# Value product of twelve chunks in four 64x64 tiles, with part sums in two PSUM banks

## The chip, the cores and the metric

The kernel runs on one core of a Trainium2 chip. The metric is the device time of one execution in microseconds (us). Before the change the median of three runs is 507.99 us (507.67 to 508.84).

## What is computed

An attention with a decaying state (RWKV), followed by a feed-forward layer with a gated activation. Cut to what matters:

```python
# r, k, v, w: (4, 8, 768, 48); u: (8, 48)
for t in range(768):
    cur = einsum('bhd,bhe->bhde', u * k[t], v[t])
    y[t] = einsum('bhd,bhde->bhe', r[t], state + cur)
    state = w[t][..., None] * state + einsum('bhd,bhe->bhde', k[t], v[t])
x = y as (3072 tokens, 384)
h = x @ w_in                      # 384 x 2048
out = (h / (1 + exp(-1.702 * h))) @ w_out   # 2048 x 384
```

## The kernel before

**Attention in chunks.** The 3072 tokens are cut into 24 chunks of 128 tokens (six chunks a batch entry). Inside a chunk the recurrence is turned into matrices. For each of the 8 heads there is a 128x128 matrix of scores, from a scaled k and a scaled r (`kf`, `qf`, products on rows of one head each, L359). A tile `am` holds for each head a diagonal matrix (L321, ScalarE) over which VectorE lays the scores where the key's token lies before the query's (`copy_predicated` with the mask `after`, L362). So `am` is triangular: keys on partitions, queries on columns, and of the four 64x64 quarters of each head's matrix the one with late keys and early queries is zero. The output of a chunk is `v` times `am`, plus the state of the chunks before times `qf`. It lies with a head's 48 features on partitions and tokens on columns.

**The crossed chunks.** From chunk 12 on (`CROSS`), heads come in pairs p = 0 to 3, and in the pairs 2 and 3 the two heads change places, so that products with the state (L371) run as four tiles of 64 rows by 64 columns of the PE array at once. Their eight products write two PSUM tiles `ps_c`, one for each half of the rows (`r_`), two pairs in each. The value products (L377) take all 128 rows (the keys) and half of the columns, two tiles at once, and add to the same banks. ScalarE then casts each `ps_c` tile to fp32r (`hi`, L222) and VectorE subtracts to get the rest (`lo`, L223), both into `x`. The output of the crossed pairs lies crossed in `x`. GpSimd's queue moves rows inside `x` by DMA (`fill_x`), and the feed-forward products of the lower half of the rows read `x` in another order (`first_rows`).

**The feed-forward in tasks.** Tokens come in six groups of four chunks (512 tokens), and each group has 16 tasks, one for each 128 of the 2048 hidden features: 96 tasks. A task's first product is 9 matmuls of 512 columns into a PSUM tile `ph`; ScalarE makes the gelu twice (`gh`, `gf`, L471), VectorE the difference `gl` (L472); two tasks later the second product adds 9 matmuls to the three output banks `po0` to `po2`. From task 32 on each matmul is cut into two halves of 64 rows that run side by side (`on_rows`, L512). At the end of a group ScalarE copies the three banks out (`ob`, L587, in the order bank 1, 0, 2), and only then can the next group's second product start in them; its first one starts in bank 1.

**What sets the order.** The order is written out by hand: a list of tokens up to task 32 (`RAMP`), and after that `rest()`, which places the steps of each chunk (`PARTS`) against the tasks, the same for every chunk: a new chunk every four tasks. Every engine then works in that order. A chunk's value products, its split and, for the chunk after it, the state update and the diagonals (`am`) fall in one place (step 8.5 of the one, 4.5 of the other). The chunks 16 and 20 have this place in the second task of a new group, and so just ahead of the copies `ob` of the group before.

Of the kernel before, what the change touches and what calls it, by code (L numbers as in the profile page):

```python
# [21 lines left out]
P = 128  # L22
# [4 lines left out]
C = P  # L27
# [57 lines left out]
def rwkv_ffn_kernel(ctx: ExitStack, tc, wkr, vp, vrk, ub, w_in, w_out, masks, vt, uc, out):  # L85
# [26 lines left out]
    after = cp.tile([P, C], F32, name="after")  # L112
# [5 lines left out]
    after_b = after.bitcast(I32).unsqueeze(1).broadcast_to([P, NP, C])  # L118
    u_heads = hm[:, 2:].rearrange("r (p h) -> r p h", h=2)
# [24 lines left out]

    def load(t):

        assert t < 2 or loaded.get(t - 2, [None])[0] is None
        a, v = lands[t % 2], values[t % 3]
        loaded[t] = [a[0:R2], v]
        first, last = (TOP if t == 0 else 0), (R2 if t % (NT - 1) == 0 else P)  # L150
        rows = wkr.rearrange("t r w -> (t r) w")[t * R + first - TOP : t * R + last - TOP]
        n = NP * CW + 1
        if t < CROSS:
            for c0, c1 in ((0, n), (n, a.shape[1])) if t < 2 else ((0, a.shape[1]),):
                if c0:
                    yield
                behind_moves(queue[0].dma_start(a[first:last, c0:c1], rows[:, c0:c1]))
        else:
            for c0, w in ((1, CW), (n, C), (n + NP * C, C)):
                for odd in range(2):  # L160
                    cols = slice(c0 + odd * 2 * w, c0 + (odd + 1) * 2 * w)
                    for half in range(2):
                        dst, src = TOP + half * D, (half ^ odd) * D
                        queue[0].dma_start(a[dst : dst + D, cols], wkr[t, src : src + D, cols])  # L164
        yield
        assert t < 3 or t - 3 in weighed
        queue[0].dma_start(v[:, TOP:], vrk[t, :, 0:DM])
        if t >= WHOLE:
            rk = pools["late"].tile([P, 2 * DM], F32, tag="rk", name="rk_t")
            queue[0].dma_start(rk, vrk[t, :, DM:])  # L170
            loaded[t].append(rk)
        yield
# [66 lines left out]
    def chunk(t):  # L239
# [7 lines left out]
        first, final = t % CB == 0, (t + 1) % CB == 0  # L247

# [24 lines left out]
        V.tensor_tensor(kf, k, li[:, :, 1:CW], op=ALU.mult)  # L273
# [37 lines left out]
        cross = t >= CROSS  # L311
# [49 lines left out]
        for h in range(2):  # L361
            V.copy_predicated(am[h], after_b, ps[h])  # L362
        yield
        cs = slice(col * C, (col + 1) * C)
        if cross:
            ps = [ps_a.tile([R2, 2, C], F32, tag="psa", name=f"ps_c{r_}") for r_ in range(2)]
            each = [(p, r_, r_ ^ p // 2) for p in (0, 2, 1, 3) for r_ in range(2)]
            if sf is not None:
                for p, r_, o in each:
                    c = p * D  # L370
                    T.matmul(  # L371
                        ps[r_][head(o), p % 2], sf[head(r_), c + o * TOP : c + HB], qf[head(r_), p],
                        start=p in (0, 2), stop=False, skip_group_check=True,
                    )
            for p, r_, o in each:
                c = (2 * p + o) * D
                T.matmul(  # L377
                    ps[r_][head(o), p % 2], v[:, c + o * TOP : c + HB], am[r_][:, p],
                    start=sf is None and p in (0, 2), stop=p in (1, 3), skip_group_check=True,
                )  # L380
# [39 lines left out]
    def fill_x(x, c0, c1, cross=False):  # L420

        for m in range(NM):
            for i, dst in enumerate((R2, 0)):
                j = TOP * (2 * m + i + 1)
                move = G.dma_start(  # L425
                    x[dst : dst + TOP, :, m ^ 2 * (cross and i == 0), c0:c1].bitcast(F32),
                    x[j : j + TOP, :, NM ^ 2 * (cross and j >= HB), c0:c1].bitcast(F32),
# [17 lines left out]
    def first_product(j, task):  # L445
# [5 lines left out]
        x = xs.get((i, 0), xs[i])  # L451
# [69 lines left out]
    def first_rows(j, half):  # L521
# [5 lines left out]
        for n in range(3 * NM):  # L527
# [5 lines left out]
                half, ("h", j), parts[j], w, xs[i][:, x, c ^ 2 * (half and starts[i] >= CROSS), cs],  # L533
# [47 lines left out]
    def store(i, start, N, order=range(NM)):  # L581
# [12 lines left out]
        xs.pop((i, 0), None)  # L594
# [5 lines left out]
    with tc.manual_schedule():  # L600
# [17 lines left out]
        def do(token):  # L618
# [7 lines left out]
            elif kind == "x":  # L626
                group, col = where[i]
                if col == CHUNKS[group] - 1:
                    fill_x(xs[group], 0, (col + 1) * C, i >= CROSS)
            elif kind == "c":  # L630
                x = xs[i, 0] = new_x(i)
                for c in range(NM):
                    for rows, src in ((slice(0, HB), c), (slice(HB, P), c ^ 2)):
                        G.dma_start(x[rows, :, c].bitcast(F32), xs[i][rows, :, src].bitcast(F32))
            elif kind == "u":
                nc.sync.dma_start(u_sb, ub)
                for x in crossed:
                    G.memset(x, 0.0)
            elif kind == "M":
# [19 lines left out]
        def rest():  # L659
# [18 lines left out]
            for j in range(FIRST, len(TASKS) + LAG):  # L678
                for post in range(2):
                    if post and j == len(TASKS) - WHOLE:  # L680
                        yield f"c{len(CHUNKS) - 1}"
# [140 lines left out]
```

## Time and profile before

| | before |
|---|---|
| median of three runs | 507.99 us |
| the profiled execution, its own time | 508.05 us |
| span of the profiled execution | 506.10 us |
| TensorE matmul busy (PE) | 494.2 us, 98% |
| VectorE (DVE) | 290.6 us, 57% |
| ScalarE (ACT) | 283.9 us, 56% |
| GpSimd (POOL) | 95.5 us, 19% |
| mean granted clock of TensorE | 0.997 of full speed |

The span is the stretch from the first to the last instruction; the execution's own time is 1.95 us longer. PE is TensorE's matmuls, PEld its loads of weights, which run beside the matmuls. An fp32 matmul shows as two rows in the trace (it runs in two passes), an fp32r matmul as one. Matmuls in different tiles of the array overlap, and a row's duration has the way through the array in it, so that the spacing of the starts and not the duration is the cost. Idle time counts where it lies on the engine that sets the end.

### The profile page before, as it was taken

How to read it: one execution, taken by the hardware profiler on the slowest of the kernel's cores; microseconds unless marked ns; L12 is line 12 of the kernel's file. 1: busy time of each engine (PE TensorE's matmuls, PEld its weight loads, DVE VectorE, ACT ScalarE, POOL GpSimd, SP SyncE). 2: the span in 40 equal slices, each digit the busy share in tenths (PEclk: the TensorE clock that was granted, in tenths of full speed). 3: DMA queues.
4: the chain of work that ended last, by engine and by line, in shares of the span. 5: the costliest groups of instructions: out<-in, count | busy, mean ns of one | idle time of the engine just before them, and what ended most of it. 6: DMA issues, size and time to landing. Idle time of an engine off the chain costs nothing.

```text
span 506.1 us, 11444 instructions
## 1 busy us (share of the span) xinstructions
PE 494.2 (98%) x4535; PEld 416.5 (82%) x4535; DVE 290.6 (57%) x451; ACT 283.9 (56%) x618; POOL 95.5 (19%) x200
## 2 busy tenths in 40 slices
PE   7999999999999999999999999999999999999994
PEld 3766777888888888888888888888888888888873
DVE  7899999999987213656456555555555322111210
ACT  4987889978865533465455465554564533323222
POOL 2002000000100200076304376303460002210000
PEclk9999999999999999999999999999999999999998
DMA  8996960125465300045112245111350001140001
GB/s 269 308 378 188 332 218 7 58 93 189 127 181 126 84 1 1 0 132 138 32 49 48 79 115 153 42 40 33 96 156 2 1 1 33 69 121 1 1 1 69
DMA packets 19471, 50.30 MB, mean 99 GB/s; under 512 B 4545, under 2 KB 8321, under 8 KB 19409
## 3 DMA queue, kind: packets, MB, share of 16 engines
q1 hardware_dynamic: 11664, 31.24, 19.3%
q0 software_dynamic: 7344, 17.72, 13.7%
q8 instruction: 38, 0.62, 0.5%
q10 hardware_dynamic: 400, 0.53, 0.3%
q14 instruction: 25, 0.20, 0.1%
HBM read 40.82 MB, written 4.72 MB: 90 GB/s over the span
## 4 chain that ended last, share of the span: by engine, by line
PE 82%; DVE 5%; ACT 4%; DMA 2%; issue 1%; POOL 1%; SPq 0%; ACTq 0%; DVEq 0%
PE po L512 26%; PE ph L512 24%; PE ps_s L359 3%; PE po L486 3%; PE ph L454 3%; PE po L487 3%; PE po L488 3%; PE ph L455 3%; PE ph L456 3%; PE ps_c L377 2%; DMA raw<-in_w_in 2%; PE ps_y L399 1%; PE ps_u L332 1%; PE ps_c L371 1%; PE ps_y L407 1%
## 5 line engine op out<-in xcount | busy, mean ns | idle before, releaser
L512 PE MATMUL ph<-x,pair 64*128 64x512 f32 x1134 | 185.5, 376 | 0.0
L472 DVE TENSOR_TENSOR gl<-gf,gh 128x512 fp32r<-128x512 f32 x96 | 66.3, 690 | 183.5 <-ACT gf L471 182.7
L512 PE MATMUL po<-gh,pair 64*128 64x512 f32 x768 | 157.6, 384 | 0.2 <-SPq L517 0.2
L512 PEld LDWEIGHTS ph<-x,pair 64*128 64x128 f32 x1134 | 143.5, 186 | 14.1
L471 ACT ACTIVATE gh<-ph 128x512 fp32r<-128x512 f32 x84 | 50.1, 597 | 157.7 <-PE ph L512 137.0
L512 PEld LDWEIGHTS po<-gh,pair 64*128 64x128 f32 x768 | 95.7, 186 | 10.4 <-issue 1.1
L512 PE MATMUL po<-gl,pair 64*128 64x512 f32 x384 | 99.2, 376 | 0.0
L425 POOL DMA_DIRECT2D x<-x x36 | 18.2, 512 | 248.5 <-DVE x L223 207.4
L321 ACT ACTIVATE am<-ident,s 128x128 f32<-128x128 f32 x192 | 58.8, 396 | 2.5 <-issue 1.5
L164 POOL DMA_DIRECT2D wkr_t<-in_wkr x108 | 53.8, 505 | 10.9 <-DVE kq L273 6.2
L512 PEld LDWEIGHTS po<-gl,pair 64*128 64x128 f32 x384 | 50.0, 186 | 4.8
L471 ACT ACTIVATE gf<-ph 128x512 f32<-128x512 f32 x84 | 49.8, 593 | 0.0
L454 PE MATMUL ph<-x,pair 128*128 128x512 f32 x99 | 39.0, 394 | 0.4 <-ACT gf L467 0.4
L456 PE MATMUL ph<-x,pair 128*128 128x512 f32 x99 | 38.0, 384 | 0.2 <-DVE pair L213 0.2
L455 PE MATMUL ph<-x,pair 128*128 128x512 f32 x99 | 37.9, 383 | 0.0
L486 PE MATMUL po<-gh,pair 128*128 128x512 f32 x96 | 37.8, 394 | 0.0
L488 PE MATMUL po<-gl,pair 128*128 128x512 f32 x96 | 36.9, 385 | 0.0
L487 PE MATMUL po<-gh,pair 128*128 128x512 f32 x96 | 36.8, 383 | 0.0
L228 ACT ACTIVATE junk<-lp 112x1032 bf16<-112x1032 f32 x24 | 25.6, 1068 | 12.3 <-DVE lp L258 12.2
L252 DVE TENSOR_TENSOR_SCAN lp<-wkr_t,d1r 112x516 f32<-112x516 f32 x24 | 29.4, 1225 | 1.3 <-DMA wkr_t<-in_wkr 1.0
L258 DVE TENSOR_TENSOR_SCAN lp<-wkr_t,d1f 112x516 f32<-112x516 f32 x24 | 29.4, 1225 | 0.1
L362 DVE COPY_PREDICATED am<-after,ps_s 128x512 f32<-128x512 int32 x40 | 26.9, 727 | 1.4 <-PE ps_s L359 1.2
(92 smaller groups left out, 645.0 us busy)
## 6 DMA issues: line engine op xcount, KB each, us to landing
wkr_t<-in_wkr SPq DMA_DIRECT2D x10, 770.5 KB, 5.3
raw<-in_w_out SPq DMA_DIRECT2D x6, 1024.0 KB, 11.4
raw<-in_w_in SPq DMA_DIRECT2D x5, 1024.0 KB, 10.9
wkr_t<-in_wkr POOLq DMA_DIRECT2D x72, 48.0 KB, 2.1
rk_t<-in_vrk POOLq DMA_DIRECT2D x9, 384.0 KB, 3.5
out_t<-ob POOLq DMA_DIRECT2D x12, 256.0 KB, 2.7
v_t<-in_vrk SPq DMA_DIRECT2D x15, 192.0 KB, 4.6
rk_t<-in_vrk SPq DMA_DIRECT2D x7, 384.0 KB, 3.4
```

The lines of the kernel that those rows point to most:

```text
L164: queue[0].dma_start(a[dst : dst + D, cols], wkr[t, src : src + D, cols])
L252: V.tensor_tensor_scan(li.rearrange("r p c -> r (p c)")[:, ::-1], w1[:, ::-1], d1r.rearrange("r p c -> r (p c)")[:, ::-1], 0.0, op0=ALU.mu ...
L321: A.activation(x_[:, p], ident, AF.Copy, scale=s[:, j : j + 1])
L454: T.matmul(o, h_, halves(x[:, 0, c, cs], plain), start=c == 0, stop=False)
L455: T.matmul(o, h_, halves(x[:, 1, c, cs], plain), start=False, stop=False)
L456: T.matmul(o, l_, halves(x[:, 0, c, cs], plain), start=False, stop=c == NM - 1)
L471: A.activation(g, ph, AF.Gelu_apprx_sigmoid, scale=1.0 / W_SCALE)
L472: V.tensor_tensor(gl, gf, gh.bitcast(F32), op=ALU.subtract)
L486: T.matmul(o, h_, halves(gh, plain), start=first, stop=False, skip_group_check=True)
L487: T.matmul(o, l_, halves(gh, plain), start=False, stop=False, skip_group_check=True)
L488: T.matmul(o, h_, halves(gl, plain), start=False, stop=f == NF - 1, skip_group_check=True)
L512: mm = T.matmul(by_twos(out), w[rows], halves(x[rows]), start=start, stop=stop, skip_group_check=True)
```

## The change

From chunk 12 on the value products are cut into tiles of 64 keys by one head's columns, four tiles at once, and the quarter that is zero is left out: for each pair and head one product of 128 columns and one of 64 instead of one of 128 columns over all keys. All products with the keys in one half of the rows write one bank, so `ps_c` is now a full bank for each half of the rows, and an output is the sum of two banks. So that both halves have the same work, the pairs 2 and 3 have their keys turned: the upper 64 tokens on the lower partitions. For this `kf` is written with its halves swapped, `am` starts from a turned diagonal (`turned`) and a mask of two halves (`after_x`), and `v`, `r` and `k` by tokens are loaded with their halves swapped for these pairs (`bring`, three DMAs for one). The heads' rows are loaded with six DMAs for twelve. The sum is made in `yt`: ScalarE copies half of the pairs from each bank, VectorE adds the parts of the other bank (four adds), and `split` works on the sum. `x` then has all heads in their places, so the crossed reads and the copy of the last group's `x` (token `c`, six DMAs) fall away. At token `u`, in the ramp, the new masks are made once.

```diff
@@ chunk(t), t >= CROSS
-        V.tensor_tensor(kf, k, li[:, :, 1:CW], op=ALU.mult)
+        if cross:
+            pairs_ = slice(0, NP // 2)
+            V.tensor_tensor(kf[:, pairs_], k[:, pairs_], li[:, pairs_, 1:CW], op=ALU.mult)
+            out_, *ins_ = (
+                y[:, NP // 2 :].rearrange("r p (b c) -> r p b c", b=2) for y in (kf, k, li[:, :, 1:CW])
+            )
+            V.tensor_tensor(out_[:, :, ::-1], *ins_, op=ALU.mult)
...
-                    A.activation(x_[:, p], ident, AF.Copy, scale=s[:, j : j + 1])
+                    A.activation(x_[:, p], turned if cross and p // 2 else ident, AF.Copy, scale=s[:, j : j + 1])
...
-            ps = [ps_a.tile([R2, 2, C], F32, tag="psa", name=f"ps_c{r_}") for r_ in range(2)]
+            ps = [ps_a.tile([R2, NP, C], F32, tag="psa", name=f"ps_c{r_}") for r_ in range(2)]
...
-            for p, r_, o in each:
-                c = (2 * p + o) * D
-                T.matmul(
-                    ps[r_][head(o), p % 2], v[:, c + o * TOP : c + HB], am[r_][:, p],
-                    start=sf is None and p in (0, 2), stop=p in (1, 3), skip_group_check=True,
-                )
+            for p, halves_ in ((0, (0, 1)), (2, (1, 0)), (1, (0, 1)), (3, (1, 0))):
+                for i_ in halves_:
+                    for r_ in range(2):
+                        o = r_ ^ p // 2
+                        c, rows, c0 = (2 * p + o) * D, slice(i_ * HB, (i_ + 1) * HB), HB * (i_ ^ p // 2)
+                        T.matmul(
+                            ps[i_][head(o), p, c0:], v[rows, c + o * TOP : c + HB], am[r_][rows, p, c0:],
+                            start=sf is None and p == 0, stop=p == 3, skip_group_check=True,
+                        )
...
+            yt = at.tile([R2, NP, C], F32, tag="rku", name="yt")
             for b, y in enumerate(ps):
-                split(*(xs[i][0:R2, n_, 2 * b : 2 * b + 2, cs] for n_ in range(2)), y)
+                two = slice(2 * b, 2 * b + 2)
+                A.copy(yt[:, two], y[:, two])
+            for b, y in enumerate(ps):
+                two = slice(2 - 2 * b, 4 - 2 * b)
+                for rows, cols in ((slice(0, HB), slice(HB, C)), (slice(HB, R2), slice(HB if sf is None else 0, C))):
+                    V.tensor_tensor(yt[rows, two, cols], yt[rows, two, cols], y[rows, two, cols], op=ALU.add)
+            split(*(xs[i][0:R2, n_, :, cs] for n_ in range(2)), yt)
@@ do(token)
-            elif kind == "c":
-                x = xs[i, 0] = new_x(i)
-                for c in range(NM):
-                    for rows, src in ((slice(0, HB), c), (slice(HB, P), c ^ 2)):
-                        G.dma_start(x[rows, :, c].bitcast(F32), xs[i][rows, :, src].bitcast(F32))
@@ token u
-                for x in crossed:
+                for x in crossed + [turned, masked[:, 1]]:
                     G.memset(x, 0.0)
+                for h in range(2):
+                    rows, cols = (slice(i * HB, (i + 1) * HB) for i in (h, 1 - h))
+                    A.copy(turned[rows, cols], ident[rows, rows])
+                A.copy(masked[HB:, 1, 0:HB], after[HB:, HB:])
+                A.copy(masked[0:HB, 1, HB:], after[0:HB, 0:HB])
+                V.memset(masked[HB:, 1, HB:], 1.0)
```

How the engines' orders change, at three places. First ScalarE at chunk 16's split, from the gelu of task 48 on (`x<-ps_c` is the cast of `hi`, `am` the diagonals of chunk 17, `ob` the copies of the group before, `gh` the gelu of task 49). Before:

```order
L471 ACTIVATE gf<-ph 128x512
L222 CAST x<-ps_c_3453 112x2x128
L222 CAST x<-ps_c_3454 112x2x128
L321 ACTIVATE am<-ident,s 128x128 x8
L587 ACTIVATE ob<-po_2362 128x512
L587 ACTIVATE ob<-po_2388 128x512
L587 ACTIVATE ob<-po_2390 128x512
L471 ACTIVATE gh<-ph 128x512
```

After:

```order
L508 ACTIVATE gf<-ph 128x512
L418 COPY yt<-ps_c_3505 112x256
L418 COPY yt<-ps_c_3506 112x256
L238 CAST x<-yt 112x4x128
L345 ACTIVATE am<-ident,s 128x128 x2
L345 ACTIVATE am<-turned,s 128x128 x2
L345 ACTIVATE am<-ident,s 128x128 x2
L345 ACTIVATE am<-turned,s 128x128 x2
L624 ACTIVATE ob<-po_2377 128x512
L624 ACTIVATE ob<-po_2403 128x512
L624 ACTIVATE ob<-po_2405 128x512
L508 ACTIVATE gh<-ph 128x512
```

The cast of `hi` moved behind two copies and reads their sum `yt`; the diagonals and the copies `ob` stand behind it as they stood behind the casts. Second, VectorE at the same place (`lp` is the scan of the chunk after). Before:

```order
L472 TENSOR_TENSOR gl<-gf,gh 128x512
L223 TENSOR_TENSOR x<-ps_c_3453,x 112x2x128
L223 TENSOR_TENSOR x<-ps_c_3454,x 112x2x128
L258 SCALAR_TENSOR_TENSOR lp<-wkr_t,d1f 112x516
L268 TENSOR_TENSOR rk_t<-rk_t 128x384
```

After:

```order
L509 TENSOR_TENSOR gl<-gf,gh 128x512
L422 TENSOR_TENSOR yt<-yt,ps_c_3505 64x2x64
L422 TENSOR_TENSOR yt<-yt,ps_c_3505 48x256
L422 TENSOR_TENSOR yt<-yt,ps_c_3506 64x2x64
L422 TENSOR_TENSOR yt<-yt,ps_c_3506 48x256
L239 TENSOR_TENSOR x<-yt,x 112x4x128
L275 SCALAR_TENSOR_TENSOR lp<-wkr_t,d1f 112x516
```

Four adds stand where the two subtractions stood, and one subtraction over all pairs follows. Third, TensorE at the same place, the first half of the value products. Before (after eight products with the state):

```order
L377 MATMUL ps_c_3453<-am,v_t 64x128
L377 MATMUL ps_c_3454<-am,v_t 48x128
L377 MATMUL ps_c_3453<-am,v_t 48x128
L377 MATMUL ps_c_3454<-am,v_t 64x128
```

After:

```order
L407 MATMUL ps_c_3505<-am,v_t 64x128
L407 MATMUL ps_c_3505<-am,v_t 48x128
L407 MATMUL ps_c_3506<-am,v_t 64x64
L407 MATMUL ps_c_3506<-am,v_t 48x64
L407 MATMUL ps_c_3506<-am,v_t 48x128
L407 MATMUL ps_c_3506<-am,v_t 64x128
L407 MATMUL ps_c_3505<-am,v_t 48x64
L407 MATMUL ps_c_3505<-am,v_t 64x64
```

Eight matmuls of a chunk became sixteen, half of them of 64 columns; the rest of TensorE's order is the same.

## Rows read from the trace of the kernel before

**Rows 1.** The page, part 1: busy us, share of the span, instructions.

```profile
PE 494.2 (98%) x4535; PEld 416.5 (82%) x4535; DVE 290.6 (57%) x451; ACT 283.9 (56%) x618; POOL 95.5 (19%) x200
```

**Rows 2.** The page, part 4: the chain that ended last, by engine.

```profile
PE 82%; DVE 5%; ACT 4%; DMA 2%; issue 1%; POOL 1%; SPq 0%; ACTq 0%; DVEq 0%
```

**Rows 3.** Busy time by stretch: crossed chunks, and the end (us, busy, PEclk, DMA).

```profile
231.00:420.00 189.00, 189.00 (x2112) 165.68 (x2112) 97.50 (x168) 98.89 (x239) 61.67 (x122) 1.00 0.24 62
...
498.00:502.00 4.00, 1.52 (x8) 0.98 (x6) 0.00 (x0) 1.79 (x3) 0.00 (x0) 1.00 0.45 161
```

**Rows 4.** Timeline of weight loads, chunk 16: start, us, what, [idle before].

```profile
287.81 0.43 PEld L371 LDWEIGHTS ps_c<-kq,sx 64*64 64x64 f32 x16 [0.33 <-issue]
288.41 0.85 PEld L377 LDWEIGHTS ps_c<-am,v_t 128*64 128x64 f32 x16 [0.17 <-issue]
289.42 0.30 PEld L512 LDWEIGHTS po<-gh,pair 64*128 64x128 f32 x4 [0.17 <-issue]
```

**Rows 5.** Timeline of weight loads, chunk 13.

```profile
231.71 0.85 PEld L377 LDWEIGHTS ps_c<-am,v_t 128*64 128x64 f32 x16 [0.17 <-issue]
232.52 0.60 PEld L332 LDWEIGHTS ps_u<-v_t,kt 128*48 128x48 f32 x16
233.18 0.30 PEld L512 LDWEIGHTS po<-gh,pair 64*128 64x128 f32 x4
```

**Rows 6.** Timeline of PE: a state update that comes behind L512.

```profile
213.59 0.67 PE L332 MATMUL ps_u<-v_t,kt 128*64 128x48 f32 x16
214.18 0.48 PE L512 MATMUL po<-gh,pair 64*128 64x512 f32 x2
```

**Rows 7.** Groups by shape in 232.6 to 233.1, PE: busy us, mean ns.

```profile
L332 PE MATMUL ps_u<-v_t,kt 128*64 128x48 f32 x8 | 0.6, 220 | 0.0
L332 PE MATMUL ps_u<-v_t,kt 128*48 128x48 f32 x8 | 0.5, 208 | 0.0
```

**Rows 8.** Timeline of ACT behind chunk 16.

```profile
289.53 0.65 ACT L222 CAST x<-ps_c 112x256 fp32r<-112x256 f32 x2 [1.17 <-PE ps_c L377]
290.06 2.45 ACT L321 ACTIVATE am<-ident,s 128x128 f32<-128x128 f32 x8
292.41 1.55 ACT L587 ACTIVATE ob<-po 128x512 f32<-128x512 f32 x3
```

**Rows 9.** Timeline of DVE behind chunk 16.

```profile
289.93 0.76 DVE L223 TENSOR_TENSOR x<-ps_c,x 112x256 fp32r<-112x256 f32 x2 [0.85 <-ACT x L222]
```

**Rows 10.** Groups by shape of DVE and ACT: busy us, mean ns.

```profile
L223 DVE TENSOR_TENSOR x<-ps_c,x 112x256 fp32r<-112x256 f32 x24 | 9.1, 420 | 10.1 <-ACT x L222 10.1
...
L339 DVE TENSOR_TENSOR sx<-ps_u,sx 112x192 f32<-112x192 f32 x8 | 2.8, 349 | 0.0
...
L211 ACT CAST pair<-c 128x1024 fp32r<-128x1024 f32 x12 | 12.4, 1046 | 1.4 <-DVE c L208 1.3
```

**Rows 11.** Timeline of weight loads: group 3's first second product after chunk 16.

```profile
293.04 0.18 PEld L512 LDWEIGHTS po<-gh,pair 64*128 64x128 f32 x1 [0.30 <-ACT ob L587]
```

**Rows 12.** Timeline of ACT and PE behind chunk 20, to group 4's first second product.

```profile
364.85 0.65 ACT L222 CAST x<-ps_c 112x256 fp32r<-112x256 f32 x2 [1.17 <-PE ps_c L377]
...
367.73 1.55 ACT L587 ACTIVATE ob<-po 128x512 f32<-128x512 f32 x3
...
368.55 0.38 PE L512 MATMUL po<-gh,pair 64*128 64x512 f32 x1
```

**Rows 13.** Timeline behind chunk 15: the next gelu (ACT), its difference (DVE), its use (PE).

```profile
274.73 0.60 ACT L471 ACTIVATE gh<-ph 128x512 fp32r<-128x512 f32 x1 [0.91 <-PE ph L512]
...
275.84 0.69 DVE L472 TENSOR_TENSOR gl<-gf,gh 128x512 fp32r<-128x512 f32 x1 [2.00 <-ACT gf L471]
...
279.30 0.38 PE L512 MATMUL po<-gh,pair 64*128 64x512 f32 x1
```

**Rows 14.** Timeline of POOL behind chunk 15, and of ACT in the ramp.

```profile
275.30 5.96 POOL L164 DMA_DIRECT2D wkr_t<-in_wkr  x12
...
95.57 0.53 ACT L308 COPY kt<-ps_t 128x448 f32<-128x448 f32 x1 [0.65 <-PE ps_t L307]
```

More of the change, by code (lines that the diff above doesn't have):

```diff
@@ L111, in rwkv_ffn_kernel @@
     make_identity(nc, ident)
-    after = cp.tile([P, C], F32, name="after")
+    masked = cp.tile([P, 2, C], F32, name="after")
+    after = masked[:, 0]
     G.memset(after, 1.0)
@@ L118, in rwkv_ffn_kernel @@
     after_b = after.bitcast(I32).unsqueeze(1).broadcast_to([P, NP, C])
+    after_x = masked.bitcast(I32).unsqueeze(2).broadcast_to([P, 2, NP // 2, C])
+    turned = cp.tile([P, P], F32, name="turned")
     u_heads = hm[:, 2:].rearrange("r (p h) -> r p h", h=2)
@@ L143, in behind_moves, with bring @@
         return dma
+    def bring(dst, src, turn):
+        if not turn:
+            queue[0].dma_start(dst, src)
+            return
+        dst, src = (y.rearrange("s (n q) -> s n q", q=DM) for y in (dst, src))
+        queue[0].dma_start(dst[:, :, 0 : DM // 2], src[:, :, 0 : DM // 2])
+        for h in range(2):
+            rows, others = (slice(g * HB, (g + 1) * HB) for g in (h, 1 - h))
+            queue[0].dma_start(dst[rows, :, DM // 2 :], src[others, :, DM // 2 :])
     def load(t):
@@ L158, in load @@
         else:
[L159 to L164, printed above, removed]
+            w_, kr = slice(1, n), slice(n, a.shape[1])
+            for cols, n_ in ((w_, 1), (kr, 2)):
+                dst, src = (y[:, cols].rearrange("r (n q) -> r n q", n=n_) for y in (a, wkr[t]))
+                one, two = (slice(h * dst.shape[2] // 2, (h + 1) * dst.shape[2] // 2) for h in range(2))
+                queue[0].dma_start(dst[TOP:R2, :, one], src[:, :, one])
+                for h in range(2):
+                    rows = slice(TOP + h * D, TOP + (h + 1) * D)
+                    queue[0].dma_start(dst[rows, :, two], src[(1 - h) * D : (2 - h) * D, :, two])
         yield
         assert t < 3 or t - 3 in weighed
-        queue[0].dma_start(v[:, TOP:], vrk[t, :, 0:DM])
+        bring(v[:, TOP:], vrk[t, :, 0:DM], t >= CROSS)
         if t >= WHOLE:
             rk = pools["late"].tile([P, 2 * DM], F32, tag="rk", name="rk_t")
-            queue[0].dma_start(rk, vrk[t, :, DM:])
+            bring(rk, vrk[t, :, DM:], t >= CROSS)
             loaded[t].append(rk)
@@ L361, in chunk @@
         for h in range(2):
-            V.copy_predicated(am[h], after_b, ps[h])
+            if cross:
+                V.copy_predicated(*(y.rearrange("s (a b) c -> s a b c", a=2) if y is not after_x else y for y in (am[h], after_x, ps[h])))
+            else:
+                V.copy_predicated(am[h], after_b, ps[h])
         yield
@@ L450, in first_product @@
         o = by_twos(ph, plain)
-        x = xs.get((i, 0), xs[i])
+        x = xs[i]
         for c in range(NM):
@@ L532, in first_rows @@
             on_rows(
-                half, ("h", j), parts[j], w, xs[i][:, x, c ^ 2 * (half and starts[i] >= CROSS), cs],
+                half, ("h", j), parts[j], w, xs[i][:, x, c, cs],
                 half == 0 and n == 0, half == 1 and end, half == 0 and end,
```

30 lines of the change are left out of this document (15 added, 15 removed).

## The prediction

> **What bounds the kernel now.** I read the page first. TensorE's matmuls are busy 98% of the span [rows 1] and hold 82% of the chain that ended last [rows 2]; the other engines have 5% or less of it. Then I asked for the stretch of the crossed chunks: from 231 to 420 us PE is busy 189.00 of 189.00 us at a granted clock of 1.00, while VectorE and ScalarE work about half of the time [rows 3]. So here the end moves by what PE's stream gets shorter or by what PE waits, and by nothing else. Two questions are left: how long the value products take before and after, and whether PE meets a new wait. For the first I read the weight loads, which show each stage's start and the stops between tilings [rows 4 to 6]; for the second ScalarE, VectorE and PE behind a chunk's products [rows 8 to 12].
>
> **The value products, per chunk.** L377 has 16 passes (8 fp32 matmuls, two passes each) of 128 columns. Their loads span 0.85 us and the next stage on the same tiles starts 0.81 us behind them [rows 5]: two column tiles side by side, 8 passes each, so 0.85/8, about 0.109 us a pass with the tail of the last. The state products beside them run the same 16 passes in four tiles in 0.43 us [rows 4]: again four passes of 0.109 a tile. So four tiles really run side by side. After the change each tile has 4 passes of 128 columns and 4 of 64. No row shows a pass of 64 columns. Bounds: half of 0.109, 0.054, and the full 0.109 if something other than columns sets it. The nearest row is the state update L332, whose passes have 48 columns and the same weights of 64: 16 passes, two tiles, in 0.60 us from cold to the next stage [rows 6], at most 0.07 a pass and, without the start, some 0.058. I take 0.058. A tile then needs 4 x 0.109 + 4 x 0.058 = 0.67 us instead of 8 x 0.109 = 0.87: **0.20 us less** a chunk.
>
> **The stops between tilings.** Going from one tiling to another PE stops: 0.17 us between loads at L371 to L377 and again at L377 to L512 [rows 4]. Of the 0.60 us from L371's start to L377's, four passes are 0.44 to 0.46, so such a stop costs some 0.14. L377 to L332 costs none, as both use 128x64 tiles [rows 5]. After the change the state and value products share a tiling, and the stop stands behind them. Where L512 follows directly (chunks 16, 22, 23) one stop goes: 0.20 + 0.14 = 0.34. Where L332 follows (13, 14, 15, 17, 19, 20, 21) the stop only moves: 0.20. Chunk 12 begins a batch entry, so its value products stand alone, with a stop on both sides either way: 0.20 less about 0.02. Chunk 18 stands alone too and gets a new stop before L332: 0.20 - 0.14, about 0.05. The sum is 3 x 0.34 + 7 x 0.20 + 0.18 + 0.05 = **2.6 us less** on PE.
>
> **What comes behind the products.** Before, ScalarE casts two halves from 289.53 on and begins chunk 17's diagonals at 290.06, 0.53 us later [rows 8]. After, in the fixed order: both copies, 0.65 us [rows 8]; hand-over to VectorE, 0.03 (the second row of the same pattern: the first cast ends at about 289.90, VectorE starts at 289.93 [rows 9]); four adds; hand-over back, about as much, 0.05 taken; the cast of all 512 columns; only then the diagonals. No row shows such an add. Both its operands have the kinds of L223 and L339, 420 ns for 256 columns and 349 for 192 [rows 10], so 1.1 ns a column and 0.28 us for 128 columns. Two in a row take 0.76 and not 0.84 [rows 9], so each hides 0.08: 0.20 + 0.34 + 0.20 + 0.42 = 1.16. (Bounds: 0.9 if the 256s cost little more than the 128s, 1.4 with nothing hidden.) The cast reads SBUF: between the diagonal's 0.29 a piece for 128 columns ((292.41 - 290.06)/8 [rows 8]) and 1.05 for 1024 [rows 10], some 0.58 for 512. In all 0.65 + 0.03 + 1.16 + 0.05 + 0.58 = 2.47, less the 0.53: ScalarE comes to everything behind the split **1.94 us later** (1.5 to 2.2).
>
> Where does that meet PE? *At most chunks nowhere.* Behind chunk 15 ScalarE had 0.91 us to spare before the next gelu at 274.73; it would come about 1.1 us late, while its difference is done at 276.53 and its first use on PE is at 279.30, 2.8 us later [rows 13].
>
> *At two chunks on PE's path.* Behind chunks 16 and 20 the copies `ob` stand next on ScalarE, and the next group's second product may not write its bank before the first of them. Behind chunk 16 PE already waits for it, to 293.04 [rows 11], just behind the copy that starts at 292.41 [rows 8]. Every us that ScalarE is later goes straight into this wait: **+1.94**. Behind chunk 20 the first `ob` starts at 367.73 and takes about 0.58 as behind chunk 16, so the bank is free at about 368.36 and PE comes at 368.55 without waiting [rows 12]: 0.19 to spare. The stop that moves behind the value products brings PE 0.14 later there, and a load no longer hidden costs 0.1 when PE stops: 1.94 - 0.19 - 0.14 + 0.1 = **+1.71**. The other group ends have no chunk's split just ahead of them.
>
> *The rest at nothing.* VectorE's extra 1.2 us a chunk hides in its half of idle time [rows 3]. POOL issues 12 loads of heads' rows in 5.96 us [rows 14]; six of these fall away and four others are added, so its queue ends earlier. Four small copies on ScalarE in the ramp fall into 0.65 us of waiting [rows 14], at most a few tenths go on. The token `c` was off the path. PE's stop of two us should not cost clock: from 498 to 502 PE works 1.52 of 4.00 us and the granted clock stays at 1.00, the 2.4 GHz level [rows 3].
>
> **The sum** against the profiled execution, 508.05 us (the median is 0.06 lower): 508.05 - 2.64 + 1.94 + 1.71 = **509.1 us**. With the bounds (PE's gain 2.1 to 2.8 with a 64-column pass of 0.070 to 0.054, the delay 1.5 to 2.2 twice) this case runs from 508.0 to 510.1. A measurement of this kernel can tell about 0.2% from no change, 1.0 us, so the forecast lies at the edge of "slower".
>
> **Rivals.** *Tiles in lockstep.* The 64-column products of one tile row stand in PE's order beside 128-column ones of the other row, and the next four behind them. If a tile can't run ahead of the others, or a pass of 64 columns costs as much as one of 128, a chunk takes 8 x 0.109 again, the 12 x 0.20 are lost, and the time is 508.05 - 0.24 + 3.65 = 511.5. Against it: in L332 the tile with 48 columns of weights is done in 0.5 us and its neighbour in 0.6, though they alternate in the order [rows 7], so tiles do run ahead. The Trainium skill (TensorE: Matmul & The Clock Gate, section The mechanism) says that matmuls start and end strictly in program order; by that rule this rival would hold, with the time just given. The trace speaks against the rule, so the chance is 0.15.
>
> *The chain is cheap (faster).* The two waits together are twice ScalarE's delay less 0.23 (1.94 + 1.71 = 2 x 1.94 - 0.23). If the delay is under 1.43 us they are under the 2.64 gained, and the change is faster: 505.4 if PE met no wait at all, up to 508. For it: ScalarE and VectorE are half idle, and the adds are few. Against it: the copies, the hand-over and the cast alone are 1.3 of the 2.47, and my lower bound of the delay is 1.5. Chance 0.17.
>
> *Every chunk pays.* If the late gelu reached PE too, each 0.1 us of it costs 1 us over ten chunks, 512 and more. The Trainium skill (TensorEngine Tiling (Array Packing), section PSUM Bottleneck) warns that after tiling the copy out of PSUM may become the bottleneck; taken for all chunks it gives this rival. The row shows 2.8 us to spare against some 1.1 us [rows 13]: 0.04. Another 0.04 is for what I don't see.
>
> **How the numbers follow.** The forecast's own case has 0.60: 0.28 of it within 0.2%, 0.32 above. With lockstep (slower), the cheap chain (0.13 faster, 0.04 the same), the late gelu (slower) and the rest, faster has 0.14, the same 0.35, slower 0.51. The range reaches from the middle of the cheap chain to near the lockstep case: 506.4 to 511.0.
>
> **What would show it.** The weight loads of the value products right behind those of the state, with no idle time between, and 0.67 us long; 0.17 us idle then before L332. Two waits of PE for `ob`, at the first second products of groups 3 and 4, some 1.7 to 2.2 us each, and no others. ScalarE waiting 1.2 us for VectorE in each split. Wrong it would be if the value products still took 0.87 us, or if the two waits were under 1 us, or if PE waited for a gelu's output.

## The result, and the profile after

| | before | after |
|---|---|---|
| median, 16 runs each | 507.87 us | 512.00 us (509.95 to 514.27) |
| profiled execution, its own time | 508.05 us | 510.93 us |
| its span | 506.10 us | 508.96 us |
| mean granted clock of TensorE in the profiled execution | 0.997 | 0.996 |

The ratio is 1.0078, 95% interval 1.0069 to 1.0087: slower, by 4.1 us. Forecast were 509.1 us and at most 511.0. Two questions follow: where the profiled execution's 2.9 us come from, and why most runs are longer still.

The page of the changed kernel, part 1 (busy us, share of the span, instructions):

```profile
PE 491.7 (97%) x4727; PEld 415.3 (82%) x4727; DVE 307.9 (60%) x500; ACT 291.2 (57%) x634; POOL 90.4 (18%) x178
```

PE works 2.5 us less than before [rows 1], and yet the span is 2.9 us longer: PE now stands still. Busy time by stretch (us, busy, granted clock, DMA) for the stretch of [rows 3]:

```profile
231.00:420.00 189.00, 185.29 (x2240) 163.43 (x2242) 111.88 (x206) 103.06 (x246) 62.47 (x111) 1.00 0.24 64
```

It was 189.00 of 189.00; now 3.71 us are idle. The weight loads of chunk 16 on the timeline (start, us, what, [idle before <- who ended it]), from its state products to group 3's first second product:

```profile
286.99 0.42 PEld L398 LDWEIGHTS ps_c<-kq,sx 64*64 64x64 f32 x16 [0.33 <-issue]
287.37 0.80 PEld L407 LDWEIGHTS ps_c<-am,v_t 64*48 64x48 f32 x32
288.26 0.30 PEld L549 LDWEIGHTS po<-gh,pair 64*128 64x128 f32 x4
...
294.13 0.18 PEld L549 LDWEIGHTS po<-gh,pair 64*128 64x128 f32 x1 [2.55 <-ACT ob L624]
```

From the first load of the state products to the first load of `po` it is 1.27 us; it was 1.61 [rows 4]. No idle time stands between L398 and L407 any more, and the whole chunk begins at 286.99 and not at 287.81 [rows 4], four times 0.20 earlier. Then comes the loss: the load at 294.13 waited 2.55 us for `ob`, where it had been 0.30 [rows 11]. Behind that wait, ScalarE and VectorE on the timeline:

```profile
288.40 0.65 ACT L418 COPY yt<-ps_c 112x256 f32<-112x256 f32 x2 [0.86 <-PE ps_c L407]
290.63 0.62 ACT L238 CAST x<-yt 112x512 fp32r<-112x512 f32 x1 [1.58 <-issue]
291.15 0.69 ACT L345 ACTIVATE am<-ident,s 128x128 f32<-128x128 f32 x2
...
293.50 1.53 ACT L624 ACTIVATE ob<-po 128x512 f32<-128x512 f32 x3
```

```profile
289.08 1.47 DVE L422 TENSOR_TENSOR yt<-yt,ps_c 64x128 f32<-64x128 f32 x4 [0.81 <-ACT yt L418]
291.28 0.69 DVE L239 TENSOR_TENSOR x<-yt,x 112x512 fp32r<-112x512 f32 x1 [0.73 <-ACT x L238]
```

ScalarE sits 1.58 us between its copies and its cast: VectorE's four additions (1.47 us) and the hand-overs ahead of them and behind them (0.03 and 0.08). From the first copy to the first diagonal are 2.75 us (291.15 - 288.40), before 0.53 [rows 8]: 2.22 us later. Behind chunk 20 the same rows give 2.75 us again, and this stop (weight loads):

```profile
370.91 0.18 PEld L549 LDWEIGHTS po<-gh,pair 64*128 64x128 f32 x1 [1.96 <-ACT ob L624]
```

A third stop was not foreseen (weight loads):

```profile
427.19 0.30 PEld L549 LDWEIGHTS po<-gh,pair 64*128 64x128 f32 x4 [0.85 <-SPq L554]
```

Its releaser is SyncE's queue: L554 is the note that a row tile of a bank is done, which on_rows passes on through SyncE. What held that queue up stands in the waits of SyncE from 420 to 430 us (in total, times, longest), first of the changed kernel, then of the kernel before:

```profile
SPq L752 <- DVE acc L749: 1.3, 1, 1.3
```

```profile
SPq L717 <- DVE acc L714: 0.3, 1, 0.3
```

L752 loads a count into a register: how many of the values that the kernel tests lie within its limits, by which it chooses between its fast path and another one. L749 copies that count from PSUM on VectorE. The notes stand behind L752. VectorE's timeline after and before shows why the count is late:

```profile
423.10 1.45 DVE L422 TENSOR_TENSOR yt<-yt,ps_c 64x128 f32<-64x128 f32 x4 [0.82 <-ACT yt L418]
425.28 0.69 DVE L239 TENSOR_TENSOR x<-yt,x 112x512 fp32r<-112x512 f32 x1 [0.74 <-ACT x L238]
426.00 0.15 DVE L749 CAST acc<-ps_n 1x1 int32<-1x1 f32 x1
```

```profile
421.20 0.76 DVE L223 TENSOR_TENSOR x<-ps_c,x 112x256 fp32r<-112x256 f32 x2 [0.85 <-ACT x L222]
422.42 0.15 DVE L714 CAST acc<-ps_n 1x1 int32<-1x1 f32 x1 [0.46 <-PE ps_n L712]
```

The copy stands in VectorE's order behind chunk 23's split, which now ends at 426.0.

**A ledger.** The profiles of all these kernels reach chunk 12 at anything from 200.0 to 202.1 us, so I compare stretches of PE: from the first weight load of one chunk's score products (L359 before, L383 after) to the next chunk's, the last one to the end of the last matmul. "e3" is the experiment below in which all three stops are gone.

| stretch that begins with the scores of chunk | before | after | e3 |
|---|---|---|---|
| 12 | 17.12 | 16.93 | 16.93 |
| 13, 14, 15 | 19.00 each | 18.80 each | 18.80 each |
| 16 (stop for `ob`) | 18.42 | 20.32 | 18.10 |
| 17 | 19.20 | 19.01 | 19.01 |
| 18 | 18.40 | 18.35 | 18.35 |
| 19 | 19.00 | 18.80 | 18.80 |
| 20 and 21 (stop for `ob`) | 19.00 + 19.00 | 20.62 + 19.01 | 18.80 + 18.80 |
| 22 | 18.25 | 17.90 | 17.90 |
| 23, to the end (stop for SyncE) | 93.29 | 93.66 | 92.95 |

Before to e3 the column falls by 2.64 us. After against e3: +2.22, +2.03 and +0.71 for the three stops, in all +4.96. So the last matmul of the changed kernel should come 2.32 us later; it came at 501.82 for 499.52. The other 0.57 us of the span lie behind the last matmul (7.15 us for 6.58); profiles of the kernels below have 6.6 to 7.4 there, so I lay nothing of it to the change.

**Why the median is above the profiled run.** Of the 16 runs eleven have a mean granted clock of 0.992 to 0.994, and a mean time of 512.5 us; the five at 0.995 to 0.997, the profiled one among them, have 510.9. So somewhere TensorE seems to fall to 1.2 GHz in most runs, at a price of 1.6 us. Where and why the experiments had to tell.

### The profile page after: what moved, and what is told of

It is laid out like the page before. It is cut to its first block, busy times and chain, and to the rows that moved or that the text cites. A ratio compares the mean times of both kernels' runs of the same rounds, so it can differ in the third digit from the quotient of the medians.

```text
span 509.0 us, 11896 instructions
## 1 busy us (share of the span) xinstructions
PE 491.7 (97%) x4727; PEld 415.3 (82%) x4727; DVE 307.9 (60%) x500; ACT 291.2 (57%) x634; POOL 90.4 (18%) x178
## 5 line engine op out<-in xcount | busy, mean ns | idle before, releaser
L549 PE MATMUL po<-gl,pair 64*128 64x512 f32 x384 | 100.4, 376 | 0.0
L549 PEld LDWEIGHTS po<-gl,pair 64*128 64x128 f32 x384 | 51.1, 186 | 4.8
L345 ACT ACTIVATE am<-ident,s 128x128 f32<-128x128 f32 x144 | 45.8, 394 | 3.0 <-issue 1.5
L244 ACT ACTIVATE junk<-kq 112x1024 bf16<-112x1024 f32 x24 | 25.4, 1059 | 1.6 <-DVE kq L299 1.6
L538 PE MATMUL idle<-d1r 112*128 112x512 bf16 x78 | 20.8, 407 | 3.1 <-POOL v_t L679 3.1
```

What stands on the lines that cost most here:

```text
L244: A.activation(junk[:, 0 : x.shape[1]], x, AF.Square, accum_out=acc[0:R2, i : i + 1])
L345: A.activation(x_[:, p], turned if cross and p // 2 else ident, AF.Copy, scale=s[:, j : j + 1])
L549: mm = T.matmul(by_twos(out), w[rows], halves(x[rows]), start=start, stop=stop, skip_group_check=True)
```

## The experiments

Theory A: the three stops are the whole loss, and one of the long ones costs clock. Against it stood the theories that the 64x64 products cost the clock (B) or that it was the chip of that day (C).

**e0: the changed kernel again.**

> The changed kernel once more, for a second profile and the clock of each run. Theory A (the two stops of TensorE of some 2.2 us behind chunks 16 and 20 are what the change costs, and in most runs the clock falls to 1.2 GHz behind one of them): 511 to 514 us, a mean granted clock near 0.993 in most runs, and in a profile of such a run the stretch behind 294 or 370 us at a clock below 1. Theory B (the many small 64x64 products draw less from TensorE and lower the clock by themselves): the same time, but the low clock lies in the stages of the value products, all twelve of them. Theory C (the chip of that day): the runs of the kernel before have the low clock too and stand above 509 us.

Measured: 511.93 us, ratio 1.0074 (1.0055 to 1.0093), clocks 0.992, 0.992, 0.996, 0.997. The runs of the kernel before beside it had 0.996 to 0.998, so C falls. The profile shows the same stops, at full clock.

**e1: the split of chunks 16 and 20 behind the output copies.**

```
-            split(*(xs[i][0:R2, n_, :, cs] for n_ in range(2)), yt)
+            parts_ = [xs[i][0:R2, n_, :, cs] for n_ in range(2)]
+            if t in (16, 20):
+                behind_store.append(lambda: split(*parts_, yt))
+            else:
+                split(*parts_, yt)
...
+                    while behind_store:
+                        behind_store.pop(0)()
```

The last two lines stand right behind the call that stores a group.

> The changed kernel with the split of chunks 16 and 20 (CAST by ScalarE and subtraction by VectorE) moved behind the three output copies ob; the four additions stay where they are. Theory A: both stops go back to what they were before the change (0.3 us behind chunk 16, none behind chunk 20), so the span falls from 508.96 by 2.26 and 2.03 to about 504.7 us, the time is 506.0 to 507.2 us, and the mean granted clock is 0.996 or 0.997 in nearly all runs. Theory B: the stops go, but the clock stays near 0.993, and the time is 507.5 to 509 us. Rival D (the late output copies are set by VectorE's masks and not by the split in ScalarE's queue): less than half of the 4.3 us comes back, 509 us or more. The third stop, of 0.7 us behind 427 us, should remain.

Measured: 506.38 us, ratio to the kernel before 0.9966 (0.9951 to 0.9980); clocks 0.997 to 0.999 in all nine runs. 5.6 us came back from 4.25 us of stops. D falls, and B loses its ground: the 64x64 products are all still there. The third stop stayed, 0.46 us of PE.

**e2: the check's count later on VectorE.**

```
+        subs[j] = V.tensor_tensor(gl, gf, gh.bitcast(F32), op=ALU.subtract)
...
+    told_ = V.tensor_copy(cnt, ps)
+    tc.add_manual_dep(told_.ins, subs[88].ins.name, SYNC, reason="the check's value is told later")
```

> The changed kernel with the copy of the check's count on VectorE told to stand behind the last but few subtractions of the gelu's low parts, far behind chunk 23, so that SyncE's load of that count no longer waits ahead of the notes on finished row tiles. Theory A (the third stop comes from SyncE's blocked queue): the stop at 427.2 us goes, the two others stay, and the profiled span falls by about 0.7 us; the time is 510.2 to 511.6 us with the clock as in the unchanged kernel. Rival E (PE would have waited there for something else, the longer split of chunk 23): no difference that can be measured against the unchanged kernel, 511 to 513 us, and another releaser is named there.

Measured: 512.60 us, ratio 1.0080 (1.0062 to 1.0099). The third stop went: the last stretch of the ledger is 92.95 us instead of 93.66, 0.7 us less as forecast, so rival E falls. The total doesn't show it, and as a time the expectation is a miss: five of the six runs were at 0.993 or 0.994. But this time the profile caught the clock. Busy time by stretch of e2 around the stop behind chunk 16 (the granted clock is the number ahead of the DMA share):

```profile
292.70:294.90 2.20, 0.06 (x3) 0.03 (x2) 1.61 (x3) 2.20 (x8) 0.00 (x0) 1.00 0.00 0
294.90:295.90 1.00, 1.00 (x11) 0.95 (x13) 0.00 (x0) 1.00 (x3) 0.78 (x2) 0.91 0.00 0
296.00:299.00 3.00, 3.00 (x23) 2.71 (x23) 2.19 (x4) 1.79 (x4) 2.97 (x6) 0.50 0.80 275
...
300.00:320.00 20.00, 20.00 (x246) 18.13 (x243) 10.21 (x18) 10.61 (x26) 13.12 (x23) 1.00 0.45 118
```

During the stop the clock is 1.00. It falls to 0.50, the 1.2 GHz level, about 0.8 us after PE has started again, for some 3 us. The two stretches of the ledger it touches are 20.31 + 20.67 us, for 20.32 + 19.01 in the changed kernel's own profile: the fall costs 1.65 us. The same place in e0's profile, where it didn't fall:

```profile
292.80:295.00 2.20, 0.05 (x3) 0.03 (x2) 1.60 (x3) 2.20 (x8) 0.00 (x0) 1.00 0.00 0
295.00:299.00 4.00, 4.00 (x46) 3.66 (x48) 2.10 (x4) 2.89 (x6) 3.79 (x7) 1.00 0.57 202
```

**e3: both edits of e1 and e2.**

> The changed kernel with both edits: the split of chunks 16 and 20 behind the output copies, and the count of the check told late. Theory A: all three stops are gone, the span is 504.0 us (508.96 less 2.26, 2.03 and 0.7), the time 505.2 to 506.6 us, faster than the kernel before by 0.3 to 0.5%, with a mean clock of 0.997. Theory B: the clock stays near 0.993 and the time is 507 to 508.5 us, no gain on the kernel before. Rival E: as the split alone, 506 to 507.2 us.

Measured: **505.66 us**, ratio 0.9962 (0.9945 to 0.9979), faster than both kernels. All three stops are gone. ScalarE and the weight load behind chunk 16 on the timeline:

```profile
287.93 0.65 ACT L418 COPY yt<-ps_c 112x256 f32<-112x256 f32 x2 [0.86 <-PE ps_c L407]
288.46 0.70 ACT L345 ACTIVATE am<-ident,s 128x128 f32<-128x128 f32 x2
...
290.81 1.54 ACT L630 ACTIVATE ob<-po 128x512 f32<-128x512 f32 x3
292.24 0.62 ACT L238 CAST x<-yt 112x512 fp32r<-112x512 f32 x1
```

```profile
291.44 0.18 PEld L555 LDWEIGHTS po<-gh,pair 64*128 64x128 f32 x1 [0.34 <-ACT ob L630]
```

The wait is back at the 0.30 of the kernel before [rows 11]. The prediction's sum without its two waits is 508.05 - 2.64 = 505.41.

**e4: the kernel before, with late output copies and nothing else.**

```
+            if part is diagonal and t in (17, 21):
+                junk = at.tile([R2, 2 * NP * CW], BF16, tag="junk", name="junk")
+                for n_ in range(4):
+                    A.copy(junk[:, 0 : NP * CW], d1r.rearrange("r p c -> r (p c)"))
```

> The kernel before, with none of the new products: ScalarE alone does four more copies of 112x516 numbers into a tile that nobody reads, between the diagonals and the output copies of group 3 (behind chunk 16) and of group 4 (behind chunk 20), some 1.9 to 2.2 us at the 0.48 us from one output copy to the next. Theory A (a late output copy stops TensorE by the delay, less what slack there is, and the stop behind chunk 16 then costs clock in most runs): the stops are 1.9 to 2.2 us behind chunk 16 and 1.6 to 2.0 us behind chunk 20, the span grows by about 4 us and by some 1.6 us more where the clock falls: 511.5 to 514.5 us, most runs at a granted clock of 0.993 or 0.994. Theory B (the clock falls because of the 64x64 products): the clock stays at 0.997 in all runs and the time is 511.5 to 512.3 us. Rival F (the stops can be caught up, since matmul work waits elsewhere for other engines): under 510.5 us.

Measured: 512.90 us, ratio 1.0112 (1.0089 to 1.0136). The stops are 2.38 and 1.93 us of PE, and the ledger's stretches grow by 2.48 and 2.40 us: a late `ob` alone does it, and nothing of it is caught up (F falls). On the clock A missed: the long stop held 0.997 or 0.998 in four of six runs.

**e5 and e6: one stop each.** e1 with `t in (20,)` (the stop behind chunk 16 stays) and with `t in (16,)` (the one behind chunk 20 stays).

> The changed kernel with only chunk 20's split behind the output copies, so that the stop behind chunk 16 (2.15 us without a matmul) stays and the one behind chunk 20 goes. If the stop behind chunk 16 is the one that costs clock (one profile shows the clock at 0.50 there from 296 to 299 us): about 2.0 us less than the changed kernel, 509.5 to 510.8 us, with 0.993 or 0.994 in most runs. If it was the one behind chunk 20: 0.997 in nearly all runs, 508.5 to 509.5 us.

> The changed kernel with only chunk 16's split behind the output copies: the stop behind chunk 20 (1.55 us without a matmul) stays. If the longer stop behind chunk 16 is the one that costs clock: 2.26 us and the clock's 1.6 us in most runs come back, 508.0 to 509.0 us, at 0.996 to 0.998 in nearly all runs. If a stop of 1.55 us costs clock too: 509.3 to 510.8 us, with 0.993 or 0.994 in most runs.

Measured: e5 510.80 us, ratio 1.0036 (1.0018 to 1.0054), ten of eleven runs at 0.994 or 0.995, and 0.56 behind the stop in its profile; e6 508.69 us, ratio 1.0013 (1.0001 to 1.0024), twelve runs at 0.995 to 0.999. Against e1 the stop behind chunk 16 (2.15 us without a matmul) costs 4.4 us by the medians, which are of different chips, and 3.6 by the ratios to the kernel before beside each; the one behind chunk 20 (1.55 us) 2.3 or 2.4. The profiles put 2.22 and 2.03 of that on the stops; the rest, and the clocks, say that the clock is lost behind chunk 16.

**e7: no additions in chunks 16 and 20** (the output lacks the part sums of the other bank there).

```
             for b, y in enumerate(ps):
                 two = slice(2 - 2 * b, 4 - 2 * b)
+                if t in (16, 20):
+                    continue
```

> The changed kernel without VectorE's four additions of part sums in chunks 16 and 20 alone (the output lacks these parts there); copies, split and order stay. It measures what the additions are worth in ScalarE's queue ahead of the output copies. By the prediction's price the stops shrink by 1.16 us each; by the rows of the changed kernel, where the four additions take 1.47 us from the first start to the last end, and the split's CAST waits for all four, by 1.4 to 1.5 us each: the stop behind chunk 16 falls from 2.15 to about 0.7 us of PE, that behind chunk 20 from 1.55 to about 0.1 us, the clock no longer falls, and the time is 507.2 to 509.0 us. If the masks or diagonals set the start of the output copies, less than half a microsecond goes from each stop, and the time stays above 510.5 us.

Measured: 507.98 us, ratio 0.9996 (0.9983 to 1.0010), clocks 0.996 to 0.998. The stretch of chunk 16 falls from 20.32 to 18.77 us, those of chunks 20 and 21 from 39.63 to 38.08: the additions with their hand-overs are worth 1.55 us each time, where the prediction had 0.03 + 1.16 + 0.05 = 1.24. ScalarE on e7's timeline:

```profile
288.67 0.65 ACT L418 COPY yt<-ps_c 112x256 f32<-112x256 f32 x2 [0.86 <-PE ps_c L407]
289.34 0.62 ACT L238 CAST x<-yt 112x512 fp32r<-112x512 f32 x1
289.87 0.69 ACT L345 ACTIVATE am<-ident,s 128x128 f32<-128x128 f32 x2
```

From first copy to first diagonal 1.20 us here, 2.75 with the additions.

**e8, e9, e10: is it the products that cost the clock?** The same block of copies as in e4 at `t == 17` alone: four in e1's kernel (e8), four in the kernel before (e9), seven in the kernel before (e10).

> The changed kernel with the split of chunks 16 and 20 behind the output copies (no stop left at either), and then four copies into a tile that nobody reads ahead of group 3's output copies alone: one stop of 2.1 to 2.5 us behind chunk 16, now from the added copies (0.64 us each in the last profile of such a run), with the 64x64 products ahead of it. It tells whether the clock that is lost behind such a stop depends on the products. Theory A' (the stop and the shorter products ahead of it together lower the clock): most runs at 0.995 or lower, 508.7 to 510.8 us. Rival G (the products play no part; it is the additions and the split, or chance): the clock is held in most runs, as it was in four of six runs of the kernel before with such copies, and the time is 508.0 to 509.0 us.

> The kernel before with the four copies ahead of group 3's output copies alone: a stop of 2.38 us behind chunk 16 with the former products (1.09 us in place of 0.83) ahead of it. Theory A' : the clock is held in most runs (0.996 to 0.998), and the time is 508.1 plus 2.4, 510.0 to 511.2 us. Rival G: the clock behaves here as in the other kernel with the same copies.

> The kernel before with seven copies in place of four at that one place: a stop of 4.2 to 4.4 us. If any long enough stop lowers the clock, whatever the products ahead of it: 0.995 or lower in nearly all runs, and 508.1 plus 4.3 plus some 1.6 us, 513.2 to 515 us. If former products keep the clock up through any such stop: 0.996 to 0.998 and 511.9 to 513.0 us.

Measured:

| kernel | stop behind chunk 16, us of PE | runs at 0.994 or less | median us, ratio (95%) |
|---|---|---|---|
| before, all runs with clocks | none | 0 of 64 (lowest 0.996) | |
| e1, e3 | none | 0 of 17 | |
| e7 (the stop cut to 0.60) | 0.60 | 0 of 10 | |
| e6 (stop of 1.55 behind chunk 20 alone) | none | 0 of 12 | |
| after, e0, e2 | 2.15 | 18 of 26 | (above) |
| e5 | 2.15 | 5 of 11, 5 more at 0.995 | |
| e11, below | 1.94 | 4 of 5 | (below) |
| e8: 64x64 products | 2.42 | 2 of 6, 1 more at 0.995 | 510.10, 1.0050 (1.0034 to 1.0066) |
| e9: former products | 2.39 | 3 of 6 | 511.94, 1.0073 (1.0056 to 1.0091) |
| e4: former products | 2.38 | 1 of 6, 1 more at 0.995 | (above) |
| e10: former products | 4.34 | 5 of 5 | 515.37, 1.0151 (1.0137 to 1.0165) |

None of the 103 runs in the first four rows is at 0.994 or less, so the count is made there. A mean of 0.995 tells neither way: two of e3's eight runs have it without a stop, for the mean holds the end of the span too, and there the clock falls too (in the changed kernel's profile it is at 0.50 from 505.2 us on, the last matmul ending at 501.82).

The former products don't protect the clock; stretches of e9 and of e10 around the stop:

```profile
294.00:296.40 2.40, 0.01 (x1) 0.00 (x0) 0.00 (x0) 2.34 (x5) 0.00 (x0) 0.95 0.00 0
296.40:299.40 3.00, 3.00 (x22) 2.82 (x24) 0.71 (x2) 2.94 (x6) 2.76 (x6) 0.50 0.51 187
```

```profile
292.50:296.90 4.40, 0.06 (x3) 0.01 (x2) 0.00 (x0) 4.24 (x8) 0.00 (x0) 1.00 0.00 0
297.00:300.00 3.00, 3.00 (x23) 2.82 (x24) 0.83 (x2) 2.83 (x6) 2.87 (x6) 0.50 0.54 199
```

So theory B falls, and A' with it: with the same copies the clock fell in two or three of six runs with either products, and e9's profile shows it at 0.50. (By its time alone e8 would lie in the range of A' and above that of G; what tells them apart is that e8 and e9 have the same clocks.) A stop is enough; at some 2 us it is hit or missed from run to run. Behind the added copies it fell less often (6 of 18 runs, 8 with those at 0.995) than behind the changed kernel's own stop; whether something else near that stop adds to it, six runs each can't tell. It stays open.

The time of e9 fits: its profile has stretches longer by 4.0 us (21.18 + 20.46 for 18.42 + 19.20), of which a fall is 1.65; with the fall in half of the runs that makes 3.2 us, and the median is 4.2 above the kernel before (2.8 to 4.6). The time of e10 does not: 6.1 us by its profile (23.12 + 20.60), 7.6 by the median (7.0 to 8.4), which is above the 515 us expected. Its other runs have clocks down to 0.990; whether the clock fell twice in them no profile shows.

**e11: the additions sorted by rows.**

```
-            for b, y in enumerate(ps):
-                two = slice(2 - 2 * b, 4 - 2 * b)
-                for rows, cols in (...):
+            for rows, cols in (...):
+                for b, y in enumerate(ps):
+                    two = slice(2 - 2 * b, 4 - 2 * b)
                     V.tensor_tensor(yt[rows, two, cols], yt[rows, two, cols], y[rows, two, cols], op=ALU.add)
```

> The changed kernel with its four additions in another order: both that write rows 0 to 63 first, then both that write rows 64 to 111, where they alternated. In the changed kernel each addition started 14 to 31 ns after the end of the one ahead of it, while two subtractions of all 112 rows overlapped by 82 ns in the kernel before (start to start 342 ns at 424 ns each). Theory H (an addition that begins at another row than the one ahead of it waits for that one's end; one at the same row starts before it): the second and the fourth start some 80 ns before the end of the first and the third, the four take about 1.27 us in place of 1.47, the stops of TensorE shrink by 0.2 us each, and the time is 511 to 513 us, no difference that a measurement of the whole can tell. Rival I (additions that read and write one tile never overlap, whatever the rows): the four take 1.47 us as before. The Trainium skill (VectorE: DVE Perf Modes, section Two Vector instructions with no wait between them) holds an instruction back until all earlier ones have finished where its inputs or output begin in another quadrant of partitions than those of the one ahead; by that rule theory H holds.

Measured: 512.34 us, ratio 1.0074 (1.0045 to 1.0104), four of five runs at 0.993 or 0.994. VectorE on its timeline:

```profile
289.77 1.25 DVE L422 TENSOR_TENSOR yt<-yt,ps_c 64x128 f32<-64x128 f32 x4 [0.82 <-ACT yt L418]
```

1.25 us instead of 1.47: the second addition starts 73 ns before the first one's end, the fourth 81 ns before the third's, while the third, which changes rows, starts 14 ns after the second's end. The stop's stretch is 20.11 us for 20.32, and 20.41 for 20.62 behind chunk 20. Theory H holds, rival I falls. That the overlapping pairs also read different banks doesn't explain it: in both kernels the third addition reads another bank than the second, begins at other rows, and overlaps by nothing.

## Why the prediction was wrong

**Right, within 0.02 us a chunk: the gain on PE.** Forecast were 0.20 us in chunks 13, 14, 15, 17, 19, 20 and 21, 0.34 in 16, 22 and 23, about 0.18 in 12 and 0.05 in 18, in all 2.65, which the sum took as 2.64. The ledger from before to e3 has 0.19 or 0.20, 0.32 to 0.35, 0.19 and 0.05, in all 2.64. A pass of 64 columns at 0.058 us was right, with some luck, as L332 [rows 6], from which it was read, has passes of 48 columns; and so was the stop that goes where L512 follows [rows 4]. Two of the signs that the prediction named for it came out otherwise: the weight loads of chunk 16's value products span 0.80 us and not 0.67, as they begin while the state products still run, and behind chunk 20 they end 0.09 us before those of the state update and not 0.17. The gain is read from the stretches of the ledger. Tiles do run ahead of one another; the rival of the lockstep falls, and with it, as the prediction said, what the Trainium skill (TensorE: Matmul & The Clock Gate, section The mechanism) would have made of it.

**Right: where PE waits for `ob`**, behind chunks 16 and 20 and nowhere else, and that no gelu reached PE.

**Mis-sized: "each hides 0.08".** "Two in a row take 0.76 and not 0.84, so each hides 0.08: 0.20 + 0.34 + 0.20 + 0.42 = 1.16." The pair it was read from are two subtractions of the same 112 rows [rows 9]; the additions alternate between two sets of rows. They took 1.47 us, more than the prediction's upper bound of 1.4, in which nothing is hidden, because 14 to 31 ns pass between one addition's end and the next one's start. With the hand-over back (0.08 for 0.05) and the cast, behind which the diagonals began sooner than priced (0.52 for 0.58), ScalarE came 2.22 us later and not 1.94, and the stops cost 2.22 and 2.03 and not 1.94 and 1.71: 0.6 us. The durations themselves (280 and 425 ns in the trace, for 0.28 and 0.42) were right. The Trainium skill (VectorE: DVE Perf Modes, section Two Vector instructions with no wait between them) has the rule: an instruction is held until all earlier ones have finished, where its operands begin in another quadrant of partitions than the last one's. e11 agrees: the additions that begin at the same rows as the one ahead overlapped by 73 and 81 ns, the one that changes rows by nothing.

**Missing: the third wait.** "Two waits of PE for `ob` ... and no others." The longer split of chunk 23 delayed a copy of one number on VectorE, that the load of it on SyncE, and that the notes behind it in SyncE's queue, for which PE waits: 0.71 us. The prediction followed ScalarE's queue behind the split, but of VectorE it said only that the "extra 1.2 us a chunk hides in its half of idle time", without listing what stands next on VectorE and who waits for that.

**Failed: "PE's stop of two us should not cost clock."** It rested on a stretch from 498 to 502 us with PE at 1.52 of 4.00 us and a clock of 1.00 [rows 3]. That row ends before the price is due. In e2 the clock is 1.00 all through the stop and falls about 0.8 us after the matmuls have begun again (0.91 on the mean of that us); in e9 it falls in the last quarter of a us of the stop (0.95 over 2.4 us). The price is paid by the matmuls that follow, and behind 499.5 us none follows, so the row couldn't show it. The same trace, from there to its end, has the clock down, with no matmul left to pay for it:

```profile
502.00:506.10 4.10, 0.00 (x0) 0.00 (x0) 0.00 (x0) 0.00 (x0) 0.00 (x0) 0.59 0.16 56
```

A fall costs 1.65 us, and in the first 16 runs eleven had it, 1.1 us on the mean.

In sum: 508.05 - 2.64 + 2.22 + 2.03 + 0.71 = 510.4 us, 510.9 measured in the profiled run, where the tail behind the last matmul was 0.57 longer; with the clock's 1.1 us 512.0, the mean of the 16 runs and, as it happens, their median. The five runs that kept the clock have 510.9, which is under the 511.0 of the forecast's range by luck: the forecast's own case ended at 510.1, and 511.0 came from the case of the lockstep, which did not occur.

## What to carry to other kernels

Where a change lengthens a chain between two engines that are half idle, list for each of the two queues what stands next behind it and who waits for that, down to a load of a single number; here the same products with two splits moved behind the output copies and one copy moved back turn +0.8% into -0.4%. A stop of TensorE is paid twice where the clock falls behind it: look at the granted clock of the stretch behind it, and in the clocks of all runs, since one profile may miss it. Before pricing instructions of VectorE by a pair that overlaps, see whether they begin at the same rows as that pair does, and sort them so.

## What was not expected of the hardware

- With stops of 1.94 to 2.42 us behind the same chunk TensorE's clock fell in some runs of a kernel and not in others (18 of 26, 4 of 5, 5 to 10 of 11, 6 to 8 of 18), with 4.34 us in all five, and with 1.55 us no run of twelve is at 0.994 or less (four are at 0.995). The Trainium skill (TensorE: Matmul & The Clock Gate, section What's actually happening) lets the gate look at TensorE on a beat of its own, which does not start anew with a kernel; a stop that is hit in one run and missed in the next agrees with that.
- The fall comes at the end of the stop or after it (in e9 ahead of the first matmul, in e2 0.8 us behind it), and the clock then stays at 0.50 for some 3 us, while PE is fully busy.
- Four additions on VectorE took 1.47 us in one order and 1.25 in another: neighbours that begin at the same rows overlapped by 73 and 81 ns, those that begin at others by nothing.
